# Halving the width of the first matmuls on ones, and one ScalarE copy at the end

## The chip, the core and the metric

The kernel runs on one core of a Trainium2 chip. Its engines work side by side: TensorE (matmuls; its weight loads are a row of their own, PEld), VectorE (DVE), ScalarE (ACT), GpSimd (POOL) and SyncE (SP), which issues most of the DMAs. The metric is the time of one execution on the device in microseconds. Times before: 307.87, 308.15 and 308.34, median 308.15.

## The reference, cut to what matters

x has 2048 rows of 640 numbers in bf16. The output is x plus attention in a sliding window on the normalised x, plus a gated feed-forward part on the normalised x:

```
xn  = layernorm(x)
qkv = xn @ wqkv                       # 32 heads of 20
p   = softmax(mask(q k^T * 20**-0.5)) # each row sees the last 256 rows, itself included
A   = (p v) @ wo
B   = (sigmoid(xn @ w_gate) * (xn @ w_up)) @ w_down   # 1536 wide
out = x + A + B
```

## The kernel before, in words

The 2048 rows are worked in four chunks of 512 rows, each of four blocks of 128. For a chunk the kernel normalises x and transposes it (xnT), projects q and k (pqk, L324) and v (pv, L353), computes scores (ps, L526) with an exponential on ScalarE (pT, L532) and masks on GpSimd (L543), multiplies with v (acc, L559), computes gate and up (pg, pu, L449 and L456) with a tanh on ScalarE into a tile called th (L452), and at the end of a chunk adds the down projection and the attention's output projection into one accumulator (y, L470 and L477), adds x on VectorE (L481) and stores the rows (L493). The order on each engine is the order in which the code issues the work; a small planner (class Fill) threads the dense matmuls between the attention steps.

What the change and the prediction touch lies at the two ends of the program.

At the start, SyncE issues the loads of x and of the weights (L156 and others). While these are on their way, nothing real can run on TensorE. The function keep_busy (L223 to L226) gives it matmuls whose two operands are a constant tile of ones, and whose results, in a PSUM tile called pwarm, nobody reads. Each of these matmuls has its own weight load of 128x128. L228 and L229 issue eleven of them, in two tiles. L683 issues two more between the transposes of block 0 and those of block 1.

Behind them come the real steps of the first chunk, in the order of L670 to L707. VectorE normalises block 0 (L252, L258, L650, L271); TensorE transposes it in five matmuls of 128 columns (pt, L277); ScalarE copies the result out (L278, called with act). ScalarE works on the mean and the squares of block 1 (L656, L661, L662), VectorE finishes its normalisation (L666, L667), TensorE transposes it and starts on the v projection (L353).

At the end, the last block of 128 rows is stored in three cuts of 320, 256 and 64 columns, on the queues of ScalarE, SyncE and ScalarE (L812 to L817). The program closes with a barrier of all engines (the rows of L841). SyncE comes to it after it has waited for all stores to land.

Also used below: L221 and L708, where ScalarE loads its tables for the square root and the exponential, and L330, ScalarE's copy of a k projection from PSUM, 128x512 from f32 to bf16.

Of the kernel before, what the change touches and what calls it, by code (L numbers as in the profile page):

```python
# [9 lines left out]
P = 128  # L10
# [7 lines left out]
CW = 512  # L18
# [20 lines left out]
FP32 = mybir.dt.float32  # L39
# [54 lines left out]
def kernel(  # L94
# [11 lines left out]
    nc = tc.nc  # L106
# [4 lines left out]
    def pool(name, bufs, **kw):  # L111
        return ctx.enter_context(tc.tile_pool(name=name, bufs=bufs, **kw))
# [13 lines left out]
    tp = pool("tp", 2)  # L126
# [22 lines left out]
    ones = nc.const_aps.tensor(1.0, [P, CW], BF16)  # L149
# [73 lines left out]
    def keep_busy(widths):  # L223
        ps = ps_d.tile([P, CW], FP32, name="pwarm", tag="d")
        for n in widths:
            nc.tensor.matmul(ps[:, 0:n], lhsT=ones[:, 0:P], rhs=ones[:, 0:n], start=True, stop=True)  # L226

    keep_busy((CW,) * 6)  # L228
    keep_busy((CW,) * 4 + (CW // 2,))  # L229

# [242 lines left out]
    def add_wo(c, s, y, cut):  # L475
        for m in range(DC):
            nc.tensor.matmul(y[:, 0:cut[1] - cut[0]], lhsT=oc[c, m][:, s * P:(s + 1) * P],  # L477
                             rhs=wo[:, m, cut[0]:cut[1]], start=False, stop=(m == DC - 1))

    def add_x(y, cut, rows):  # L480
        nc.vector.scalar_tensor_tensor(  # L481
            out=rows[:, cut[0]:cut[1]], in0=y[:, 0:cut[1] - cut[0]], scalar=0.5,
            in1=rows[:, cut[0]:cut[1]], op0=MULT, op1=ADD)
# [7 lines left out]
    def store(c, s, rows, cut=(0, D), queue=nc.sync):  # L491
        sb = c * SBC + s
        queue.dma_start(out=out2[sb * P:(sb + 1) * P, cut[0]:cut[1]], in_=rows[:, cut[0]:cut[1]])  # L493
# [301 lines left out]
    def add_down(s, cut, home, tag):  # L795
        ys[s, cut] = home.tile([P, CW], FP32, name="y0", tag=tag)
        run(down(c, s, ys[s, cut], cut))
# [14 lines left out]
    for cut, queue in zip(cuts, (nc.scalar, nc.sync, nc.scalar)):  # L812
        if cut == cuts[2]:
            add_down(last, cut, ps_y, "y")
        add_wo(c, last, ys[last, cut], cut)
        add_x(ys[last, cut], cut, rows[last])
        store(c, last, rows[last], cut, queue)  # L817
# [1 line left out]
_INS = ['A_x', 'A_wqkv', 'A_wo', 'B_x', 'B_w_gate', 'B_w_up', 'B_w_down']  # L819
_OUTS = [((1, 2048, 640), 'bfloat16')]  # L820
# [25 lines left out]
```

## Time and profile before

| | us |
|---|---|
| median of three runs | 308.15 (307.87 to 308.34) |
| the profiled execution | 308.24 |
| its span, first to last instruction | 306.4 |
| TensorE busy | 302.0 |
| ScalarE busy | 198.5 |
| first matmul on ones starts | 0.84 |
| the eleventh ends | 5.00 |
| last compute instruction (VectorE, L481) starts | 303.59 |

Times inside the profile count from the first instruction. The profiled execution takes 1.8 us more than its span, which lies around it. Engines are named PE, PEld, DVE, ACT, POOL and SP; a q behind the name (SPq, ACTq) marks instructions that the engine's queue handles and that do not count as busy, such as DMA issues, waits for a semaphore and drains. A row such as "out<-in 128x512" names what an instruction writes and reads; "<-DVE xn L271" behind a time in brackets tells how long the engine stood idle before it, and what ended that. A chain lists the work that ended last, each step released by the one before.

### The profile page before, as it was taken

Reading aid. Unit: us, or ns where it says so; the run is one execution under the profiler, and the core shown is the slowest. Engines: PE = TensorE matmul, PEld = TensorE weight load, DVE = VectorE, ACT = ScalarE, POOL = GpSimd, SP = SyncE. Lnnn points to the kernel's source line nnn. Section 1 sums busy time; section 2 is a strip of 40 time slices with the busy share of each in tenths; the row PEclk is TensorE's granted clock in tenths of the full one; section 3 lists DMA queues with packets and bytes.
Section 4 is the critical chain, followed back from the end, with each engine's and each line's share of the span. In section 5 each row is a group of like instructions: output and inputs, shape, how many; then the busy total and the mean of one; then the engine's idle time right before and its main releaser. Section 6 shows DMA issues by size and latency. Waiting matters only on the chain.

```text
span 306.4 us, 10028 instructions
## 1 busy us (share of the span) xinstructions
PE 302.0 (99%) x4314; PEld 164.8 (54%) x4314; DVE 177.7 (58%) x355; ACT 198.5 (65%) x197; POOL 177.5 (58%) x317
## 2 busy tenths in 40 slices
PE   7999999999999999999999999999999999999996
PEld 3654444445657644554457654554546664444774
DVE  5735539879675564497946464483733526372534
ACT  6933877698854649888674647878585547778000
POOL 3174686787982828576682728557382847557000
PEclk9999999999999999999999999999999999999999
DMA  7998987986537062810036212740000210000202
GB/s 206 361 325 266 303 199 213 318 229 192 175 97 166 21 180 70 273 40 2 2 132 131 66 58 87 231 144 0 2 2 2 71 40 25 2 2 2 88 21 68
DMA packets 40174, 36.87 MB, mean 120 GB/s; under 512 B 8864, under 2 KB 39840, under 8 KB 40096
## 3 DMA queue, kind: packets, MB, share of 16 engines
q1 hardware_dynamic: 39264, 35.46, 38.2%
q10 hardware_dynamic: 864, 0.75, 0.8%
q8 instruction: 34, 0.56, 0.8%
q14 instruction: 12, 0.10, 0.1%
HBM read 25.59 MB, written 11.44 MB: 121 GB/s over the span
## 4 chain that ended last, share of the span: by engine, by line
PE 97%; DMA 1%; ACT 1%; DVE 0%; SPq 0%; issue 0%
PE y L470 18%; PE pu L456 18%; PE pg L449 17%; PE pqk L324 15%; PE ps L526 9%; PE pv L353 7%; PE y L477 7%; PE acc L559 6%; DMA xc<-in_A_x_dram 1%; PE pt L277 0%; ACT xn L656 0%; ACT xn L661 0%; DVE xn L667 0%; SPq L156 0%; ACT rstd L662 0%
## 5 line engine op out<-in xcount | busy, mean ns | idle before, releaser
L543 POOL TENSOR_SCALAR_AFFINE_SELECT pT<-pT 64x512 bf16<-64x512 bf16 (+1 forms) x256 | 157.4, 615 | 83.0 <-ACT pT L532 70.5
L532 ACT ACTIVATE pT<-ps 128x2048 bf16<-128x2048 f32 (+1 forms) x76 | 141.0, 1855 | 59.4 <-PE ps L526 56.0
L460 DVE SCALAR_TENSOR_TENSOR h<-th,pu 128x512 bf16<-128x512 f32 x48 | 32.6, 680 | 49.7 <-PE pu L456 44.2
L456 PE MATMUL pu<-xnT,wu 128*128 128x512 bf16 x240 | 59.8, 380 | 0.0
L449 PE MATMUL pg<-xnT,wg 128*128 128x512 bf16 x240 | 59.8, 380 | 0.0
L470 PE MATMUL y<-wd,h 128*128 128x320 bf16 (+2 forms) x396 | 56.6, 295 | 0.0
L470 PEld LDWEIGHTS <-h 128*128 128x128 bf16 x396 | 36.7, 98 | 15.8 <-issue 1.8
L452 ACT ACTIVATE th<-pg 128x512 f32<-128x512 f32 x48 | 28.6, 595 | 15.5 <-PE pg L449 15.4
L449 PEld LDWEIGHTS <-wg 128*128 128x128 bf16 x240 | 22.2, 98 | 25.8 <-issue 1.8
L456 PEld LDWEIGHTS <-wu 128*128 128x128 bf16 x240 | 22.0, 98 | 25.5 <-issue 2.0
L526 PE MATMUL ps<-qT,kT 20*64 20x320 bf16 (+4 forms) x1440 | 32.1, 260 | 0.0
L571 DVE STREAM_TRANSPOSE t<-acc 128x512 f32<-128x512 f32 x32 | 21.1, 696 | 17.3 <-PE acc L559 17.3
L526 PEld LDWEIGHTS <-kT 20*64 20x64 bf16 x1440 | 15.4, 103 | 25.0 <-issue 22.4
L481 DVE SCALAR_TENSOR_TENSOR rows<-y,rows 128x320 bf16<-128x320 f32 x30 | 14.5, 488 | 22.8 <-PE y L477 22.7
L583 DVE TENSOR_TENSOR on<-t,rec 128x320 bf16<-128x320 f32 (+4 forms) x48 | 26.1, 543 | 1.1
L353 PE MATMUL pv<-wv,xnT 128*128 128x320 bf16 x160 | 25.7, 300 | 0.0
L477 PE MATMUL y<-wo,oc 128*128 128x320 bf16 (+2 forms) x165 | 24.2, 295 | 0.0
L324 PE MATMUL pqk<-xnT,wq 128*128 128x512 bf16 x100 | 23.2, 380 | 0.0
L324 PE MATMUL pqk<-xnT,wk 128*128 128x512 bf16 x100 | 23.1, 380 | 0.0
L364 DVE CAST v<-pv 64x320 bf16<-64x320 f32 x29 | 14.1, 486 | 11.7 <-PE pv L353 11.4
L559 PE MATMUL acc<-pT,v 64*32 64x320 bf16 (+4 forms) x1440 | 19.6, 253 | 0.0
L559 PEld LDWEIGHTS <-v 64*32 64x32 bf16 x1440 | 16.2, 91 | 5.8 <-issue 1.6
(53 smaller groups left out, 194.7 us busy)
## 6 DMA issues: line engine op xcount, KB each, us to landing
qT<-sq SPq DMA_DIRECT2D x16, 256.0 KB
kT<-sk SPq DMA_DIRECT2D x16, 256.0 KB
sq<-st SPq DMA_DIRECT2D x20, 128.0 KB
sk<-st SPq DMA_DIRECT2D x20, 128.0 KB
out_dram<-rows SPq DMA_DIRECT2D x15, 160.0 KB
wg<-in_B_w_gate_dram SPq DMA_DIRECT2D x4, 480.0 KB
wu<-in_B_w_up_dram SPq DMA_DIRECT2D x4, 480.0 KB
xc<-in_A_x_dram SPq DMA_DIRECT2D x3, 640.0 KB
```

Of the source, the lines that this page charges most:

```text
L324: nc.tensor.matmul(ps, lhsT=wt[:, m, :], rhs=xnT[c][:, d, :], start=(d == 0), stop=(d == DC - 1))
L353: nc.tensor.matmul(ps[:, 0:HALF], lhsT=xnT[c][:, d, s * P:(s + 1) * P], rhs=wqkv[2][:, d, hf * HALF:(hf + 1) * HALF], start=(d == 0), stop ...
L449: nc.tensor.matmul(pg, lhsT=part(wg, d, f), rhs=xnT[c][:, d, :], start=(d == 0), stop=(d == DC - 1))
L452: nc.scalar.activation(out=th, in_=pg, func=TANH, scale=0.5)
L456: nc.tensor.matmul(pu, lhsT=part(wu, d, f), rhs=xnT[c][:, d, :], start=(d == 0), stop=(d == DC - 1))
L460: nc.vector.scalar_tensor_tensor(out=h, in0=th, scalar=1.0, in1=pu, op0=ADD, op1=MULT)
L470: nc.tensor.matmul(y[:, 0:cut[1] - cut[0]], lhsT=ht[c, f][:, s * P:(s + 1) * P], rhs=wd[:, f, cut[0]:cut[1]], start=(f == 0), stop=False)
L477: nc.tensor.matmul(y[:, 0:cut[1] - cut[0]], lhsT=oc[c, m][:, s * P:(s + 1) * P], rhs=wo[:, m, cut[0]:cut[1]], start=False, stop=(m == DC - 1))
L526: nc.tensor.matmul(ps[a * U:(a + 1) * U, i, col * U:(col + n) * U], lhsT=qk["k", kc, o // GH][32 * i:32 * i + DH, o % GH + a, kb * U:(kb + ...
L532: nc.scalar.activation(out=pt[:, :, 0:width], in_=ps[:, :, 0:width], func=EXP, scale=SCALE)
L543: nc.gpsimd.affine_select(out=view, in_=view, pattern=[[0, HG], [0, n], [sign, U]], compare_op=GE, fill=0.0, base=base, channel_multiplier ...
L559: nc.tensor.matmul(acc[32 * i:32 * i + 32, q * U:(q + n) * U], lhsT=vt[kb][a * U:(a + 1) * U, u, h * VW:h * VW + 32], rhs=pt[a * U:(a + 1) ...
```

## The change

The first ten matmuls on ones take 256 columns each instead of 512 and become twenty; the eleventh, of 256 columns, stays. The two calls, and so the two tiles, remain two. At the end of the program, behind the issue of the last store, ScalarE copies the tile of ones into a new tile from the pool of the tanh results. Nothing reads that tile.

```diff
-    keep_busy((CW,) * 6)
-    keep_busy((CW,) * 4 + (CW // 2,))
+    keep_busy((CW // 2,) * 12)
+    keep_busy((CW // 2,) * 9)
...
         store(c, last, rows[last], cut, queue)
+    nc.scalar.copy(out=tp.tile([P, CW], FP32, name="th"), in_=ones)
```

CW is 512 and P is 128. The ones are bf16, the copy's result is f32.

## The prediction

> **What bounds the kernel now.** I read the page first, then the opening microseconds and the closing ones, because the two edits sit there. From the page, the span, TensorE's busy time and the chain that ended last:
>
> ```profile
> span 306.4 us, 10028 instructions
> ...
> PE 302.0 (99%) x4314; PEld 164.8 (54%) x4314; DVE 177.7 (58%) x355; ACT 198.5 (65%) x197; POOL 177.5 (58%) x317
> ...
> PE 97%; DMA 1%; ACT 1%; DVE 0%; SPq 0%; issue 0%
> ```
>
> TensorE is the chain for 97% of the span. Only what delays TensorE after its first real work, or what stretches the end behind its last matmul, can move the time. The chain, taken for the first 9 us, says when TensorE becomes the bound (start, duration, what):
>
> ```profile
> 5.98 0.46 DVE xn L667
> 6.43 0.05 issue
> 6.48 0.45 PE pt L277 x5
> 6.93 1.44 PE pv L353 x10
> ```
>
> Before 6.48 us the chain is the load of x (1.25 to 3.54), then ScalarE and VectorE normalising block 1. The matmuls on ones (L226) are not on it. The timeline of weight loads (start, duration, engine, line) gives the pace of those matmuls, since each has one load:
>
> ```profile
> 0.81 0.14 PEld L226 LDWEIGHTS <-const-bfloat16-1.0 128*128 128x128 bf16 x2 [0.81 <-issue]
> 1.22 0.15 PEld L226 LDWEIGHTS <-const-bfloat16-1.0 128*128 128x128 bf16 x1 [0.28 <-issue]
> 1.65 0.15 PEld L226 LDWEIGHTS <-const-bfloat16-1.0 128*128 128x128 bf16 x1 [0.28 <-issue]
> ...
> 4.21 0.15 PEld L226 LDWEIGHTS <-const-bfloat16-1.0 128*128 128x128 bf16 x1 [0.28 <-issue]
> 4.51 0.10 PEld L226 LDWEIGHTS <-const-bfloat16-1.0 128*128 128x128 bf16 x1 [0.15 <-issue]
> 5.34 0.28 PEld L277 LDWEIGHTS <-xn 128*128 128x128 bf16 x5 [0.73 <-DVE xn L271]
> ```
>
> See the steps: 0.43 us per matmul of 512 columns up to 4.21, then 0.30. Later the chain has fifty such matmuls (L324) in 10.79 us, 0.216 each. So TensorE starts at half speed, 1.2 columns per ns, and doubles inside the step that begins at 4.21: 0.30 = t + (512 - 1.2t)/2.4 gives t = 0.17, a rise at 4.38 us, 3.54 us after the first matmul (0.84). The page's PEclk row, nines throughout, does not show this; the spacing does. The same stretch by matmul:
>
> ```profile
> 0.84 4.16 PE L226 MATMUL pwarm<-const-bfloat16-1.0 128*128 128x512 bf16 x11 [0.84 <-PEq L830]
> 4.84 0.45 DVE L271 TENSOR_SCALAR xn<-xc,mv,rstd 128x640 bf16<-128x640 bf16 x1
> 5.35 0.45 PE L277 MATMUL pt<-ident,xn 128*128 128x128 bf16 x5 [0.34 <-DVE xn L271]
> ```
>
> The matmuls on ones are over at 5.00. The transposes that follow wait until VectorE's block 0 is done (4.84 + 0.45 = 5.29): TensorE is idle for 0.34 us.
>
> **The change, part by part.** *The matmuls on ones.* Before: ten of 512 columns and one of 256, 5,376 columns. After: 12 + 9 = 21 of 256, again 5,376. So ten matmuls and ten weight loads more, the same columns, the same two tiles; the later pair of 512 and 128 columns stays. At 1.2 columns per ns a matmul of 256 steps by 0.213 us. Its successor's load lasts 0.15 in this state, so 0.06 is left if it lies beside the matmul, as it does now: 0.15 busy and 0.28 idle make the whole step of 0.43. After the rise a step is 0.109 and a load 0.10, tighter; but the five transposes of 128 columns at 5.35, each with its own load of 98 ns, all start and end within 0.45, less than five loads in a row take (0.49). What a matmul costs beyond its columns comes from the chain: 17 of 320 columns in 2.31 us are 0.1359 each, 50 of 512 are 0.2158; the difference is 0.416 ns per column, which leaves 2.5 ns fixed. Ten more times 2.5 ns is 0.025 us. The stream ends at 5.03 instead of 5.00, against 5.29: 0.00 us on the path, hidden behind VectorE's normalisation. If that cover were gone, it would be 0.03.
>
> One rule of the Trainium skill speaks against this. TensorE: Matmul & The Clock Gate, Part 3 (The mechanism), says that weight loads overlap matmuls in flight only when they go to another row group. All loads here take the full 128 rows. The trace differs: the steps of 0.216 and 0.1359 contain a load of 0.098 each, and if loads stood ahead of matmuls the remainders (0.118 and 0.038) would not be in the ratio of 512 to 320 columns. By the row the sum is 0.00, by the rule it is the first rival below.
>
> *The rise of the clock* matters more than the matmuls do. The array is kept streaming from 0.84 to 5.0 in both versions, with equal columns at every instant, so I take the rise to stay at 4.38: 0.00 us. No row shows what a stream of shorter matmuls does to it. An earlier rise gains nothing, as TensorE would only idle longer before 5.29. A later one is bounded by a second stretch of 3.54 us, a rise at 7.92, priced below at 0.7. I take the end 0, since what is equal in the two streams, columns and time, is nearest to what this row measures.
>
> The Trainium skill, TensorE: Matmul & The Clock Gate, Part 1, says that the warm-up is counted in time, in windows of about 3.4 us that run freely, not in matmuls. The 3.54 us agree, and by it the number of matmuls is of no account.
>
> *The copy on ScalarE.* One instruction, 128x512, bf16 to f32, from SBUF, behind the last store's issue. ScalarE's nearest rows, in order of time the store it follows and then rows by line (min/median/max ns, first and last start):
>
> ```profile
> 303.85 0.35 ACTq L493 DMA_DIRECT2D out_dram<-xn  x1
> ```
>
> ```profile
> L330 ACT CAST st<-pqk x20: 580/592/654, 19.5 to 191.6; 128x512 bf16<-128x512 f32 x20
> ```
>
> ```profile
> L841 SPq EVENT_SEMAPHORE  x7: 17/28/28, 304.1 to 306.3; - x7
> ...
> L841 SPq DRAIN  x3: 7/7/13, 305.6 to 305.9; - x3
> ...
> L841 ACTq DRAIN  x2: 8/79/150, 304.2 to 306.0; - x2
> ```
>
> The price is 0.59 (the row of the same size; 0.48 for L278's 384 elements and 0.73 for L656's 640 bound it). ScalarE's issue ends at 304.20 and its drain starts at 304.2. After: copy 304.24 to 304.83, drain of 0.15 to 304.98. SyncE meanwhile waits for the stores to land and comes to its own drain only at 305.6; the closing barrier waits for it. ScalarE is 0.6 us earlier than that: 0.00 us, covered by the landing of the last stores. Without that cover it costs 0.59. Nothing is queued behind the copy but ScalarE's drain. SyncE also waits for ScalarE's count, which the copy raises by one, in its last wait together with the last store's landing, so 304.83 is early enough. The copy waits only for an earlier write of its tile, the tanh tile, whose last writer ended at 283.9, and issues no DMA.
>
> *What moves.* Apart from these, the order of instructions on every engine is unchanged; SyncE's and GpSimd's queues are the same. TensorE's program grows by 20 instructions on 8,628. Queue q8, of kind instruction, moved 34 packets of 16 KB in this run, and TensorE's waits name three causes in all, two VectorE results and the start: no wait for instructions to gain or lose.
>
> **Sum.** 308.24 us (the profiled execution: span 306.4 and 1.8 around it) + 0.00 + 0.00 + 0.00 = 308.24. It lies 0.09 above the median of 308.15 (307.87 to 308.34); I give 308.2. A measurement of this kernel can tell some 0.2%, 0.6 us, from no change.
>
> **Rivals.**
>
> 1. *Exposed weight loads, slower.* If loads cannot lie beside matmuls this short, a pair costs 0.15 + 0.213 = 0.365 at half speed: 9.8 pairs until 4.38. The other 11.2 at 0.10 + 0.109 take 2.3, and TensorE is free at 6.7, 1.35 later than the transposes now start. Of that, 0.25 is slack: ScalarE's copies of block 0 end at 6.47 and the projection that needs them starts at 6.77. So +1.1, 309.3. It decides from the point where the stream passes 5.29 by more than that slack. Against it: the loads hidden in steps of 0.136. For it: no row has a step of 0.213 or 0.109. Chance 0.05.
>
> 2. *The clock rises a stretch later, slower.* Rise at 7.92 instead of 4.38. The ones end about 5.3 (5,376/1.2 = 4.48 us), just in time. The pair of 512 and 128 columns fits before 6.48. Block 1's transposes take 0.25 longer and the projections behind them lose half of 7.02 to 7.92, 0.45: +0.7, 308.9. For it: the rise came only 0.6 us before the ones ended, so little reserve is seen. Against: equal columns. The timing at the rise may also differ from run to run in both kernels, which would not show as a difference. Chance 0.06, half of it under 0.2%.
>
> 3. *The copy reaches past the landing, slower.* It would if a table load came with it: 1.28 (L221) makes 304.24 + 1.28 + 0.59 + 0.15 = 306.26, 0.65 past 305.6, 308.9. It decides from 0.6 us of extra time. Against: ScalarE's copies at 5.72 (L278) run between a square root and a square root with no load beside them. A copy that did not run at all would give 308.2 as well. Chance 0.04.
>
> 4. *Faster.* A shift of TensorE's instruction stream might save waits. The trace has 0.75 us of TensorE idle in two waits for VectorE and none for instructions, so I know no mechanism; a gain past 0.6 would mean about 307.5. Chance 0.05.
>
> **How the numbers follow.** Forecast 0.80, rivals 0.05, 0.06, 0.04 and 0.05. Faster by over 0.2%: 0.05. Slower by over 0.2%: 0.05 + 0.03 + 0.04 = 0.12. Within: 0.83. The range goes from 307.5 (the lowest shown, 307.87, less a spread like its own distance from the median) to 308.9 (the late rise and the late copy); it leaves out the exposed loads.
>
> **What would show it.** Right: 21 loads of L226 in steps of 0.213 and then 0.109, the ones over by 5.1, block 0's transposes again released by VectorE (L271) near 5.35, the projection near 6.77; at the end a copy of about 0.59 us from 304.24, with SyncE's drain still about 1.4 us behind the end of ScalarE's last issue. Wrong: steps near 0.365, transposes released by TensorE itself, loads of 0.15 after 5 us (a late rise), a table load in the last 3 us, or a wait of SyncE that ends on ScalarE.

## The result and the profile after

| | before | after |
|---|---|---|
| median (range, executions) | 308.24 (307.87 to 309.13, 9) | 309.23 (308.75 to 310.06, 9) |
| ratio, 95% interval | | 1.0033 [1.0020, 1.0046] |
| profiled execution, its span | 308.24, 306.4 | 308.75, 307.0 |

The change costs 0.33% of the time, about 1 us. The forecast was 308.2 with a range up to 308.9: the time is outside it, on the slower side. The execution that was profiled is the fastest of the nine, so its trace shows about half of what the median lost.

The page of the changed kernel, the same lines as before and the row of the instruction queue:

```profile
span 307.0 us, 10014 instructions
...
PE 300.1 (98%) x4289; PEld 166.3 (54%) x4324; DVE 178.2 (58%) x355; ACT 199.0 (65%) x198; POOL 176.6 (58%) x317
...
q8 instruction: 34, 0.56, 0.8%
...
PE 96%; issue 1%; ACT 1%; DMA 1%; DVE 0%; SPq 0%; ACTq 0%
```

TensorE stays the chain, but "issue" has come up from 0 to 1%. 35 matmul records are missing from this trace (4289 of 4324), which leaves small holes called issue; the weight loads are complete, so the two traces are set side by side load by load. First the start, by the chain (start, duration, what) and by the weight loads:

```profile
5.91 0.46 DVE xn L667
6.37 0.05 issue
6.41 0.45 PE pt L277 x5
6.87 1.44 PE pv L353 x10
```

```profile
0.81 4.19 PEld L226 LDWEIGHTS <-const-bfloat16-1.0 128*128 128x128 bf16 x21 [0.81 <-issue]
5.27 0.28 PEld L277 LDWEIGHTS <-xn 128*128 128x128 bf16 x5 [0.28 <-DVE xn L271]
```

The 21 loads of L226 end at 5.00, and the first transposes still wait for VectorE. The first work is 0.07 us earlier than before (6.41 for 6.48). Nothing is lost here. Now the end, by ScalarE's timeline and by the rows of the closing line (min/median/max ns, first and last start):

```profile
303.96 1.12 ACTq L493 DMA_DIRECT2D out_dram<-xn  x2
305.12 0.62 ACT L818 CAST th<-const-bfloat16-1.0 128x512 f32<-128x512 bf16 x1 [20.36 <-DVE xn L481]
```

```profile
L842 SPq DRAIN  x3: 7/7/13, 306.3 to 306.6; - x3
...
L842 ACTq DRAIN  x2: 14/182/350, 305.4 to 306.6; - x2
```

The copy is over at 305.74 and ScalarE's longer drain, 0.35 from 305.43, at 305.78. SyncE comes to its drain only at 306.3. So 0.5 us is in hand, and the copy is hidden as worked out.

What is new lies in the middle. TensorE's waits (what waited for what: us in total, times, longest):

```profile
PE pwarm L226 <- PEq L831: 0.8, 1, 0.8
PE pv L353 <- issue: 0.6, 1, 0.6
PE pt L277 <- DVE xn L667: 0.4, 1, 0.4
PE pg L449 <- issue: 0.3, 2, 0.2
PE y L470 <- PE ps L526: 0.2, 1, 0.2
PE pqk L324 <- issue: 0.2, 1, 0.2
PE pu L456 <- issue: 0.2, 1, 0.2
```

Five rows of these were not there before. Three of them (pg, pqk and pu) are holes that missing matmul records leave: the weight loads keep their pace there. Two are real: a wait of 0.6 for nothing that the profile can name, and one of 0.2 whose named releaser is TensorE itself. TensorE's timeline around the longer one, near 204 us, after and then before:

```profile
203.14 0.43 PE L526 MATMUL ps<-qT,kT 20*64 20x320 bf16 x24
204.18 0.84 PE L353 MATMUL pv<-wv,xnT 128*128 128x320 bf16 x5 [0.61 <-issue]
```

```profile
202.92 0.43 PE L526 MATMUL ps<-qT,kT 20*64 20x320 bf16 x24
203.28 0.85 PE L353 MATMUL pv<-wv,xnT 128*128 128x320 bf16 x5
```

The same 24 score matmuls and the same v projection: 0.36 us from start to start before, 1.04 after. TensorE stands still for 0.68 us, and no other engine has changed its work. Standstills are given in this way from here on, as the time from start to start beyond the usual 0.36. The idle time in brackets is some 0.07 shorter. Around the shorter one, near 82 us, it is the down projection behind 24 score matmuls, again after and then before:

```profile
81.60 0.43 PE L526 MATMUL ps<-qT,kT 20*64 20x320 bf16 x24
82.25 1.38 PE L470 MATMUL y<-wd,h 128*128 128x320 bf16 x9 [0.22 <-PE ps L526]
```

```profile
81.66 0.43 PE L526 MATMUL ps<-qT,kT 20*64 20x320 bf16 x24
82.02 1.53 PE L470 MATMUL y<-wd,h 128*128 128x320 bf16 x10
```

Here it is 0.65 for 0.36: 0.29 more. Of this 0.03 is paid back a little later, because the kernel before itself loses 0.03 at 83.42. The account of this execution: -0.07 + 0.29 - 0.03 + 0.68 = +0.87 at TensorE's last instruction (0.88 measured there). The end behind the last store's issue was 0.25 us shorter in this execution, which leaves +0.6 of span.

**The theory, "Blocks".** TensorE's program is read while it runs, in packets of 16 KB on queue q8: 34 packets for 8,648 instructions, about 254 each, so I take 256. Counting with that, both standstills fall on a border, 15 blocks apart: with TensorE's loads, matmuls and semaphore waits numbered from 0 in the trace, the instruction that comes late is number 1,985 near 82 us and number 5,825 near 204 us, 3,840 or 15 times 256 later. Twenty instructions more at the start put every border on earlier work. At two places the instructions behind the border then fall due before their packet can be used. The trace's record of that packet near 204 us: it starts at 201.90 and has landed at 202.93, and TensorE resumes at 204.18; near 82 us it has landed at 80.72 and TensorE resumes at 82.25. Before, the later packet landed at 203.30 and instruction 5,825 came at 205.05; the earlier one landed at 81.92 and instruction 1,985 came at 83.42, the place of the 0.03 above. **Rivals:** the clock or the narrow matmuls at the start ("Clock"), and the copy ("Copy").

The Trainium skill, Runtime: NRT & Kernel Launch, Instruction fetch mechanics, says that the sequencer fetches the next block of 256 instructions through a DMA queue of its own while it executes the current one, and that crossing the border is mostly hidden. The packets agree (16 KB, 34 of them). That the crossing is hidden does not hold here: 0.29 and 0.68 us.

### The profile page after: what moved, and what is told of

Read it like the earlier page. It is cut to its first block, busy times and chain, and to the rows that moved or that the text cites. A ratio compares the mean times of both kernels' runs of the same rounds, so it can differ in the third digit from the quotient of the medians.

```text
span 307.0 us, 10014 instructions
## 1 busy us (share of the span) xinstructions
PE 300.1 (98%) x4289; PEld 166.3 (54%) x4324; DVE 178.2 (58%) x355; ACT 199.0 (65%) x198; POOL 176.6 (58%) x317
## 4 chain that ended last, share of the span: by engine, by line
PE 96%; issue 1%; ACT 1%; DMA 1%; DVE 0%; SPq 0%; ACTq 0%
PE y L470 18%; PE pu L456 17%; PE pg L449 17%; PE pqk L324 14%; PE ps L526 9%; PE pv L353 7%; PE y L477 7%; PE acc L559 6%; DMA xc<-in_A_x_dram 1%; PE pt L277 0%; ACT xn L656 0%; ACT xn L661 0%; ACT th L818 0%; DVE xn L667 0%; SPq L156 0%
## 5 line engine op out<-in xcount | busy, mean ns | idle before, releaser
L456 PE MATMUL pu<-xnT,wu 128*128 128x512 bf16 x228 | 59.0, 380 | 0.7 <-issue 0.2
L449 PE MATMUL pg<-xnT,wg 128*128 128x512 bf16 x226 | 58.6, 380 | 0.9 <-issue 0.3
L353 PEld LDWEIGHTS <-xnT 128*128 128x128 bf16 x160 | 14.8, 98 | 8.9 <-issue 1.4
```

The lines of the kernel that those rows point to most:

```text
L353: nc.tensor.matmul(ps[:, 0:HALF], lhsT=xnT[c][:, d, s * P:(s + 1) * P], rhs=wqkv[2][:, d, hf * HALF:(hf + 1) * HALF], start=(d == 0), stop ...
L449: nc.tensor.matmul(pg, lhsT=part(wg, d, f), rhs=xnT[c][:, d, :], start=(d == 0), stop=(d == DC - 1))
L456: nc.tensor.matmul(pu, lhsT=part(wu, d, f), rhs=xnT[c][:, d, :], start=(d == 0), stop=(d == DC - 1))
```

## The experiments

Ratios are against executions of the kernel before on the same chip, taken together with those of the experiment. Profile numbers are of one execution each.

**1. The narrow widths alone** (the change without the copy).

> The twenty-one matmuls of 256 columns alone, without the copy at the end. Theory Blocks: TensorE's program comes in blocks of 256 instructions (34 packets of 16 KB on queue q8); twenty more instructions ahead of everything move the borders between blocks to other work, and at two of them the next block is not there yet. Then the time is that of the whole change, 309.2 (+0.3%), with matmuls standing still near 82.0 us (about 0.3) and near 203.5 (about 0.65). Rival Copy: the copy at the end costs the time; then 308.2 here. Rival Clock: the narrow matmuls put off the rise of TensorE's clock; then slower by up to 0.7, but before 9 us and with no standstill later.

Measured: 309.76 (308.87 to 312.77, 10), before 308.39, 1.0050 [1.0027, 1.0074]. The trace has standstills of 0.49 at 83 us and 1.41 at 205 us, at instructions 1,985 and 5,825 again. The later one:

```profile
203.94 0.43 PE L526 MATMUL ps<-qT,kT 20*64 20x320 bf16 x24
205.71 0.70 PE L353 MATMUL pv<-wv,xnT 128*128 128x320 bf16 x4 [1.35 <-issue]
```

In this execution the clock rose only near 6.75 and delayed the start by about 0.6. The loss belongs to the matmuls on ones, not to the copy.

**2. The copy alone.**

> The wide matmuls on ones as before, and only the copy at the end. Blocks and Clock: 308.2, within 0.1% of the kernel before, no standstill of TensorE near 82 or 203 us. Copy: 308.8 to 309.2, with SyncE's last wait ended by ScalarE.

Measured: 308.14 (307.97 to 309.19, 12), 0.9998 [0.9987, 1.0010]; no standstill. "Copy" is out.

**3. The wide matmuls kept, ten short ones behind them**: the same twenty instructions more, almost no columns.

```diff
-    def keep_busy(widths):
+    def keep_busy(widths, short=0):
...
+        for _ in range(short):
+            nc.tensor.matmul(ps[0:32, 0:16], lhsT=ones[0:U, 0:32], rhs=ones[0:U, 0:16], start=True, stop=True)
...
-    keep_busy((CW,) * 4 + (CW // 2,))
+    keep_busy((CW,) * 4 + (CW // 2,), 10)
```

> The wide matmuls on ones as before, no copy, and behind the eleventh ten more matmuls on ones of 16 columns with weights of 64x32: the same twenty instructions more, but the first stretch as it was. Blocks: 309.2 with the two standstills near 82 and 203.5 us, as in the whole change. Clock: 308.2, since the wide matmuls are back. Copy: 308.2.

Measured: 310.16 (309.19 to 310.52, 6), 1.0055 [1.0034, 1.0075]. The first real work starts within 0.02 us of before's, and TensorE stands still ahead of the same two instructions, here for 0.49 and 2.15. Its timeline near 204 us:

```profile
203.42 0.43 PE L528 MATMUL ps<-qT,kT 20*64 20x320 bf16 x24
205.93 0.84 PE L355 MATMUL pv<-wv,xnT 128*128 128x320 bf16 x5 [2.08 <-DVE v L366]
```

The releaser in brackets is inferred, and here it misleads. The two copies by VectorE on the line that it names ran from 204.85 to 205.83; before, the same copies ran from 204.36 to 205.34, and the projection started ahead of them, at 203.28. "Clock" is out, since the widths are those of before and the start is too.

**4. A whole block more**: the narrow widths and 118 short matmuls in the second call, 256 instructions more in all, so that the borders fall on the same work as before.

> Twenty-one matmuls of 256 columns as in the change, no copy, and behind them 118 more of 16 columns with weights of 64x32, so that TensorE's program is longer by exactly 256 instructions than before and every border falls on the work on which it fell before. Blocks: the two standstills are gone; the time is 308.2 plus whatever the 118 short matmuls push the first transposes back, which the trace shows (118 at 13 to 27 ns are 1.5 to 3.2 us, of which 0.25 is hidden). Clock: the narrow matmuls still delay the rise, so there is a loss before 9 us beyond that push. If the standstills near 82 and 203.5 us remain, Blocks is wrong.

Measured: 312.57 (311.24 to 313.32, 5), 1.0143 [1.0121, 1.0166]. TensorE's timeline at the later place, and the chain of the start:

```profile
206.20 0.43 PE L528 MATMUL ps<-qT,kT 20*64 20x320 bf16 x24
206.56 0.85 PE L355 MATMUL pv<-wv,xnT 128*128 128x320 bf16 x5
```

```profile
0.84 4.02 PE pwarm L226 x21
4.87 3.06 PE pwarm L228 x118
```

0.36 from the scores to the projection, as before: no standstill, nor at the earlier place. The two packets had landed 2.65 and 2.53 us ahead of need. This is one execution, the fastest of the five; the others have no trace. The page has 35 packets on q8, one more. The whole loss is at the start, where the short matmuls take 3.06 us and the clock is low again behind them: the next five transposes take 0.65 us in place of 0.45 (3.28 us in all). The time itself tells nothing for or against; the places do.

**5. The change's widths, and fewer transfers ahead of the packet.** The loads that bring the second half of q and k (L342: four of 256 KB for each chunk from the second on) are issued by ScalarE after the chunk's last v copy, instead of by SyncE earlier.

```diff
-    def spread(w, c, g0, g1):
+    def spread(w, c, g0, g1, queue=nc.sync):
...
-            nc.sync.dma_start(out=qk[w, c, half][:, o:o + 2, :], in_=src[b])
+            queue.dma_start(out=qk[w, c, half][:, o:o + 2, :], in_=src[b])
...
-            if s == 1:
-                spread("q", c, GH, NG)
-                spread("k", c, GH, NG)
+            if s == SBC - 1:
+                spread("q", c, GH, NG, nc.scalar)
+                spread("k", c, GH, NG, nc.scalar)
```

> The twenty-one matmuls of 256 columns, without the copy (as in e1_widths), but the four transfers of 256 KB per chunk that bring the second half of q and k (L342) are issued by ScalarE after the chunk's last v copy instead of by SyncE after the second v block. The theory Blocks, sharpened by the first four runs: the fetch of an instruction block is served only when the data transfers queued ahead of it have drained, and TensorE goes on 1.3 to 1.5 us after it has landed; near 80 and 202 us the fetch waits for these very transfers and two loads of rows. With them out of the way the fetches of those two blocks land 1 us or more earlier, the standstills near 82 and 203.5 us go or shrink to below 0.3 in sum, and the time is 308.2 to 308.6 instead of 309.2 to 309.8. Rival: what counts is only where the border lies, and the fetch takes its time whatever else moves; then 309.2 to 309.8 as before, with the same standstills.

Measured: 308.36 (308.25 to 308.82, 11), before 308.38, 1.0003 [0.9995, 1.0012]. The DMA view from 198 to 205 us, forty slices of 0.175 us, busy tenths of the 16 DMA engines; first the whole change, then this kernel:

```profile
DMA  9996799999799999999976841010000000000000
...
q8 instruction: 1, 0.02, 0.9%
```

```profile
DMA  8999999886920000000000000000100000000400
...
q8 instruction: 2, 0.03, 2.3%
```

In the change the data keep the DMA engines full until about 202, and the packet starts as they run out (201.90). Here they run out at 200.1, the packet starts at 199.91 and has landed at 201.24, 2.6 us before instruction 5,825 is due (203.81). TensorE does not stop:

```profile
203.81 0.85 PE L353 MATMUL pv<-wv,xnT 128*128 128x320 bf16 x5
```

This execution is 0.43 us late from its start on, because the first load of x took 2.75 us in place of 2.29, and it is still within 0.2% of the kernel before. So the widths cost nothing (interval up to 0.12%) where the packet is not behind those transfers.

**6. The same move in the kernel before.**

> The kernel before with the same later issue of the second halves of q and k by ScalarE. It prices the move itself: 16 issues of 0.35 to 0.5 us on ScalarE, which has room. Blocks: 307.9 to 308.2, since the kernel before passes the same two blocks with little in hand and some of its executions are longer for it (308.39 median, 307.86 lowest). Rival: 308.4 or slower, as ScalarE's exponentials come later by an issue.

Measured: 308.51 (308.41 to 308.93, 11), 1.0002 [0.9990, 1.0015]. The expected gain did not come. Its trace loses 0.11 us near 145.7, where the product with v waits for VectorE's mask of chunk 2 (L536, over at 145.93, before at 145.32), and 0.17 at the start. The exponential ahead of that mask is no later than the start makes it (143.15 for 142.99), so the 0.18 us that the expectation of 11 puts down to it is a misreading. So the move is no gain by itself that 5 could have hidden a loss behind. None of the 11 executions was above 309, against 4 of 27 of before.

**7. The ten short matmuls from 107 us on**, two ahead of each q projection of chunk 2, so that only the later borders move.

```diff
+        for _ in range(2 if w == "q" and c == 2 else 0):
+            nc.tensor.matmul(ps[0:32, 0:16], lhsT=ones[0:U, 0:32], rhs=ones[0:U, 0:16], start=True, stop=True)
```

> The wide matmuls on ones as before, no copy, and the ten short matmuls (16 columns, weights of 64x32) not at the start but two ahead of each of the five q projections of chunk 2, from 107 us on. Blocks: the border near 82 us stays where it was and no standstill is there; the one near 203.5 is, with 0.6 to 2.1 us. Time 309 to 310.3, of which at most 0.3 is the ten matmuls' own. Rival, that more instructions at the start cost something at the start: 308.4 to 308.7.

Measured: 309.89 (309.64 to 310.32, 5), 1.0051 [1.0038, 1.0064]. Nothing is lost near 82 us, and about 0.29 inside the projection at 204.78 to 205.9, less than the 0.6 to 2.1 expected. The late instruction is number 5,825 once more, here a weight load. So the place follows the position in the program. But the ten matmuls cost 0.95 us where they stand, more than the 0.3 expected, and this execution starts 0.52 us late, as its first load of x took 2.84 us. The time therefore supports the theory less than the trace does.

**8 and 9. Three and twenty short matmuls** at the start (as in 3): 6 and 40 instructions more.

> As e3_ten_short with three short matmuls instead of ten: borders move by 6 instructions instead of 20. Blocks: a border moved by 6 is reached about 0.4 us earlier near 83 us and 0.65 earlier near 204.6, instead of 1.2 and 1.3, so the standstills are smaller: 0 to 0.3 and 0 to 1.4, and the time lies between that of the kernel before and that of ten, 308.5 to 309.3. Rival, that any border other than the old one is bad in itself: about 310 as with ten.

> As e3_ten_short with twenty short matmuls: borders move by 40 instructions. The work at the moved borders then falls due at 81.7 and 203.0 us (in the times of the kernel before), while the blocks were there for work at 82.3 to 82.5 and at 204.0 to 205.4 in the runs with ten. Blocks: standstills of 0.6 to 0.8 and of 1.0 to 2.4, a little more than with ten; time 309.8 to 311.3. If the time falls back to 308.4, or the standstills sit elsewhere, what is said of the fetches here is wrong.

Measured: three, 308.43 (307.86 to 309.11, 11), 1.0000 [0.9988, 1.0012], no standstill over 0.02; the packet landed at 203.14 and instruction 5,825 came at 204.53, 1.39 us later. The time lies just under the 308.5 to 309.3 expected. Twenty, 308.61 (308.06 to 309.05, 12), 1.0002 [0.9991, 1.0013]. The second expectation failed: more instructions lost less, 0.05 near 82 us and this near 204, where instruction 5,825 is now a score matmul and comes 0.45 us late:

```profile
203.59 0.27 PE L528 MATMUL ps<-qT,kT 20*64 20x128 bf16 x10 [0.23 <-issue]
```

I had held the arrival fixed and moved only the border. But the packet moved too: it starts at 201.02 and has landed at 202.14, 0.8 us earlier than in the change. The profile does not show when a block is asked for. So the loss does not grow with the number of instructions. That it hangs on where a border falls between the transfers is argued from this, not shown. The expectations of 8 to 10 also count from 83.1 and 204.6 us for the kernel before, where the trace has 83.42 and 205.05.

**10. Two matmuls fewer**: the kernel before without the pair of L683, borders 4 instructions later.

> The kernel before without the two matmuls on ones between the transposes of blocks 0 and 1 (L683); a reader loses nothing, their result is not read. Borders move the other way, by 4 instructions, and the two late blocks fall due 0.3 and 0.45 us later than before, at 83.4 and 205.1 us. Blocks: no standstill in any execution, time 308.0 to 308.4, the same as before or up to 0.1% faster. Rival, the missing matmuls cost TensorE its clock: slower by up to 0.7, before 13 us.

Measured: 308.72 (308.07 to 309.58, 12), 1.0018 [1.0005, 1.0030]. The expectation failed. The profiled execution (308.21) has no standstill, and its packets landed 2.63 and 2.28 us ahead of need, more than before; yet 5 of the 12 are above 309. This kernel is a little slower, the theory gives no reason for it, and its trace does not say why. It stays open.

**11 and 12. The move of 5 in chunks 1 and 3 alone**, which leaves chunk 2 as it was, in the kernel before and in the whole change.

```diff
-            if s == 1:
+            if s == (1 if c == 2 else SBC - 1):
+                queue = nc.sync if c == 2 else nc.scalar
```

> The kernel before with the later issue of the second halves of q and k by ScalarE in chunks 1 and 3 alone, where the two tight blocks are fetched; chunk 2 keeps SyncE's issue, as its move in e6_before_later_spread made an exponential late and cost 0.18 us at 145.7. Blocks: no standstill near 82 or 204 us in any execution; 308.0 to 308.3, and fewer executions above 309 than the kernel before. If it is 308.5 again, the move costs elsewhere what it saves.

> The whole change, narrow matmuls and copy, with the same later issue in chunks 1 and 3. Blocks: the change then costs nothing: the same as e11_before_later_1_3 within 0.1%, 308.0 to 308.4, with no standstill near 82 and 203.5 us. If it stays 0.2% or more above it, part of the loss of the change lies elsewhere.

Measured: in before, 308.50 (308.26 to 308.77, 11), above the 308.0 to 308.3 expected, before itself 308.42, 0.9999 [0.9986, 1.0011]; in the whole change 308.24 (308.10 to 308.71, 12), 0.9995 [0.9984, 1.0006]. The change with the move has no standstill, and TensorE's last instruction is 0.07 us from before's. The whole change, copy included, costs nothing once the packets at the two places do not stand behind these transfers. No kernel here beats the kernel before by more than the interval. The moved transfers narrow the spread (none of 23 executions above 309, against 4 of 23 of before); that the long executions of the kernel before are late blocks too was not shown.

The place near 204 us in six kernels, by the trace's packets; the third column is when instruction 5,825 came (us):

| kernel | packet starts, landed | instruction came | standstill |
|---|---|---|---|
| before | 202.21, 203.30 | 205.05 | none |
| whole change | 201.90, 202.93 | 204.18 | 0.68 |
| 1, widths | 203.14, 204.23 | 205.71 | 1.41 |
| 3, ten short | 203.48, 204.55 | 205.93 | 2.15 |
| 5, later transfers | 199.91, 201.24 | 203.81 | none |
| 9, twenty short | 201.02, 202.14 | 203.59 | 0.45 |

## Why the prediction was wrong, by its own steps

- *The matmuls on ones, 0.00*: right. 21 loads, over at 5.00, transposes at 5.28 released by VectorE. Each load of 0.147 us lies beside a step of 0.213. Loads of all 128 rows overlap here, so rival 1 is out. This is against the rule of the Trainium skill, TensorE: Matmul & The Clock Gate, Part 3 (The mechanism), that the prediction weighed and set aside.
- *The rise of the clock, kept at 4.38*: wrong in time, without effect. The loads keep 0.147 and steps of 0.213 up to the last at 4.85, so the rise came later than that. The transposes were waiting anyway. Experiment 1's execution shows what a rise near 6.75 costs (0.6), rival 2's mechanism; but the rise came near 6.2 in experiment 6, whose matmuls on ones are those of before, so it is no property of the change, and 3 has the loss without it.
- *The copy, 0.00*: right. It took 617 ns for the 590 taken, began 0.9 us later than worked out because the whole end was later, and left 0.5 us to SyncE's drain. Experiment 2: 0.9998. Rival 3 is out.
- *What moves*: **this step failed.** "TensorE's waits name three causes in all ... no wait for instructions to gain or lose." It had the twenty instructions and the 34 packets, and then took the absence of waits as proof that none could come. What the trace of before could show is how near the next packets were: 1.50 and 1.75 us between landing and need at these two borders, the least of its 33 (the next have 1.86 and 2.16), behind a burst of data. In the traces with a standstill TensorE resumes 1.25 to 1.52 us after the landing, so at most 0.25 and 0.5 us were left to give. The change brought the need forward by about 1.5 us at both borders (83.42 to 81.96 and 205.05 to 203.50), and the packets landed only 1.2 and 0.4 us earlier. This step gave the sum no term; the profiled execution measured 0.29 and 0.68 us.
- *Rival 4* named the right object, the shift of the instruction stream, and gave it one direction only, faster. The opposite was missing: a block that falls due early, at borders 256 instructions apart, and waits for a packet that lands late.
- *The range*: its lower end is 307.6 by the working given (307.87 less 0.28), not 307.5. Nothing rests on this.

Shown by experiments: the loss comes with the widths and not with the copy (1, 2); neither the widths nor the clock is needed, twenty instructions suffice (3); the place is a number of instructions and not a piece of work (1, 3, 7, 9); the standstills go when the borders return to their work (4, by one trace) and the loss goes when the transfers ahead of the packet go (5, 12). Argued only: that the median's 0.99 us, more than the 0.51 of the profiled execution, is the same standstills at larger sizes; experiments 1 and 3 show such sizes (1.41 and 2.15), the other eight executions of the change have no trace.

## What to carry to other kernels

Where an engine is the bound for nearly the whole span and its program is long, adding or removing a handful of instructions anywhere moves every later block border, and a microsecond can appear hundreds of microseconds away. Before pricing such an edit at nothing, find where the instruction queue's packets land late, beside bursts of data, and by how much ahead of need. An unnamed or odd wait at one place that comes and goes with the instruction count is best tested by adding a whole block, or by moving the transfers that stand ahead of the packet.

## What the runs showed of the hardware that was not expected

- A packet of 16 KB was not usable at its landing: TensorE resumed 1.25 to 1.52 us later (the six standstills of the change, 1 and 3; 1.33 in 7, 1.52 and 1.45 in 9).
- At these two places the packet took 0.9 to 1.4 us. Near 204 us it started as the data ran out in the change and in 5; in 9 it started at 201.02, when the DMA engines were still full, and in 3 about 1 us after the data had fallen below two tenths. The Trainium skill, DMA: Bandwidth & Descriptors, Queues, rings and completion order, has each DMA engine alternate between its queues packet by packet; here the packet of the change started near the end of a burst of 1.33 MB (window 198 to 205). What it waited for inside a DMA engine no trace here shows.
- The profile has no name for this wait: it called it "issue", TensorE's own earlier matmuls, or a VectorE copy that in the kernel before ends after the projection has started.
- Short matmuls of 16 columns with loads of their own are not cheap late in the program: ten took 0.95 us amid the projections (7), and 118 took 3.06 at the start, 26 ns each, and left the clock low (4: five transposes behind them in 0.65 us for 0.45).
